# The end of an attention and spectral-filter kernel: the last output product in three rounded terms, its stores on another queue, its last block copied in two halves

## The chip, the cores and the metric

One core of a Trainium2 chip runs the whole kernel. The metric is device time in microseconds (us), from the start to the end of one execution. The names of the engines are those of the profile: PE multiplies matrices (PEld is its load of the stationary operand), DVE is the vector engine, ACT the scalar engine, POOL is GpSimd and SP is SyncE, which here only issues DMAs and waits. A trailing q (SPq, ACTq) is the engine's instruction sequencer: DMA issues, semaphore waits, register loads and branches are its work.

## What is computed

Two independent results stand side by side in the output. One is attention with 16 query heads of width 28 that share one key and one value head, over 2048 positions; the other is a 2-D FFT of a second input, a pointwise product with a filter, and the inverse FFT. The change touches only the attention's last product:

```python
scores = jnp.einsum("bhqd,bkd->bhqk", q, k) * (Dh ** -0.5)
p = _softmax(scores, axis=-1)
o = jnp.einsum("bhqk,bkd->bhqd", p, v)
return (lambda x, *d: x.transpose(*d))(o, 0, 2, 1, 3).reshape(B, S, H * Dh) @ wo
```

All data are float32. `x @ wo` has 448 rows of `wo` and 448 columns of output.

## The kernel before, in words

The 2048 query positions are cut into `NC` = 4 chunks of `CW` = 512, the 16 heads into `NG` = 4 groups of 4 heads, 32 rows a head. For each pair (chunk `c`, group `g`) PE makes scores of 16 key blocks (line 872), ACT takes the exponentials (lines 816 and 895, with DVE copying some scores out first, line 878), and PE multiplies them with the values into one PSUM bank, with the sum of the exponentials in a spare row (`flush`, line 827). When a pair is complete, DVE transposes the bank into the SBUF tile `osb` (line 831), divides by the sums (`divide`, line 713) and transposes back.

What comes next is a product with one group's rows of `wo`. PE takes float32 operands in several passes; operands of type `F32R`, a rounded float32, in one. To keep precision with rounded operands the kernel splits a tensor into a rounded part and the rounded remainder, and adds three products: high by high, low by high, high by low. `woh` and `wol` hold the two parts of `wo`, `wox` the high part for groups 1 to 3 as it belongs to the low part of the other operand (a few spare rows of it differ). `oh[c]` and `ol[c]` hold the two parts of the divided attention output. `norm` (line 715) fills them for a pair, `wo_mm` (line 730) makes the three products, and `wo_out` (line 738) copies a finished block of 128 positions by 448 columns out of PSUM and stores it to the output `oa`. For chunks 0 to 2 and for groups 0 to 2 of chunk 3 all this is spread through the main loop or done at its end.

The order of work on PE is that of the program text from line 231 on, and that of DVE and ACT from line 493 on. SP's and POOL's instructions are put in order by the framework. Waits are set by the framework too, from what the instructions read and write.

The last pair, chunk 3 and group 3, is handled by lines 907 to 934. Its part of `wo` is loaded once more, unrounded, into the tile `w3` (lines 908 and 909, from SP's queue). `flush(kept)` makes the last products with the values. DVE then divides and transposes in four blocks of 128 positions, into the tile `on` (lines 924 to 927). PE meanwhile makes the products of groups 0 to 2 for a block, nine rounded matmuls into one PSUM bank (`partial`, line 912), and adds the last group's in float32 (`final`, line 916):

```python
for k in (0, 1):
    partial(k)
for k in (2, 3):
    final(k - 2)
    partial(k)
final(2)
final(3)
```

For these four blocks `wo_out` is called with `on_act=True`: ACT copies the block (line 741) and issues the store from its own queue (line 746).

Behind this stands a block of code for inputs whose scores exceed a bound (lines 939 to 1005). It isn't entered with these inputs. Every one of the five engines loads the value `bits` into a register (line 939) and takes the branch over that code (line 940). Past it each engine has some semaphore waits (line 940 again; on SP one for each of the five DMAs that the skipped code would issue), then the end of the program (line 1123): SP waits one after another for the semaphores of all DMA queues and engines, each engine drains, and a common barrier ends the program.

Of the kernel before, what the change touches and what calls it, by code (L numbers as in the profile page):

```python
# [10 lines left out]
F32 = mybir.dt.float32  # L11
# [3 lines left out]
AF = mybir.ActivationFunctionType  # L15
ALU = mybir.AluOpType
# [4 lines left out]
S, D, H = 2048, 448, 16  # L21
DH = D // H
DF = D // 2 + 1
NG = 4
# [38 lines left out]
def kernel(ctx: ExitStack, tc: tile.TileContext, t: dict):  # L63
    nc = tc.nc
    mm = nc.tensor.matmul
# [71 lines left out]
    def fft1_a_mm(q, p):  # L137
        f, cs1 = ff[q], fc["cs1"][:113]
        pa = pair_of(bank())
        for e in range(2):  # L140
            for k, (n, o0) in enumerate(((113, 0), (112, 113))):
                for h in range(2):
                    for r in range(2):
                        r0 = 64 * h + 32 * r
                        mm(pa[r0:r0 + 32, e, o0:o0 + n], f[:, 2 * r + k, 2 * p + e, h], cs1[:, 2 * r + k, :n],  # L145
                           start=True, stop=True)
        return pa

    def fft1_a_out(q, p, pa):
        a = at1[q, p] = fp.tile([128, 2, DF], F32, name="a", tag=("pwr", "pwi")[p])  # L150
        return nc.scalar.activation(a, pa, AF.Copy)

    def fft1_b(q):
        return fft1_out(q, fft1_mm(q))
# [92 lines left out]
    with tc.tile_pool(name="w1", bufs=1) as w1:  # L247
# [37 lines left out]
        with tc.tile_pool(name="x1", bufs=2) as x1:  # L285
# [63 lines left out]
            def evac(c, g, pq):  # L349
                cs = slice(c * CW, (c + 1) * CW)  # L350
                out = nc.scalar.activation(qraw[:, g, cs], pq, AF.Copy)
                nc.vector.tensor_reduce(qmx[:, g, c:c + 1], qraw[:, g, cs], axis=AX.X, op=ALU.max,
                                        apply_absolute_value=True)
                return out
# [55 lines left out]
            for c in range(1, NC):  # L410
                for g in range(NG):
# [3 lines left out]
                    last = evac(c, g, pq)  # L415
# [43 lines left out]
        for p in range(2):  # L459
            last = fft1_a_out(6, p, fft1_a_mm(6, p))  # L460
# [7 lines left out]
        last = fft1_b(5)  # L468
# [26 lines left out]
    d, f, a, b, e, c = free  # L495
# [14 lines left out]
    ap = pools.enter_context(tc.tile_pool(name="ap", bufs=2))  # L510
    pp = pools.enter_context(tc.tile_pool(name="pp", bufs=P_BUFS))
# [25 lines left out]
    def at_once(work=640, engine="dve"):  # L537
        clock[engine] = max(clock[engine], clock["pe"] + 200) + work

    begun = []  # L540
    woh = ap.tile([128, NG, D], F32R, name="woh", bufs=1)
    wol = ap.tile([128, NG, D], F32R, name="wol", bufs=1)

    wox = ap.tile([128, NG - 1, D], F32R, name="wox", bufs=1)

    wo = {}
# [143 lines left out]
    oh, ol, osb = {}, {}, {}  # L690
# [11 lines left out]
    def divide(c, g, k=None):  # L702

        o = osb[c, g]
        sums = o.rearrange("p (b d) -> p b d", d=32)
        if not k:
            r = osb["r"] = ap.tile([128, 16], F32, name="r", bufs=1)
            nc.vector.reciprocal(r, sums[:, :, DH])
            if c == NC - 1:
                nc.vector.memset(sums[:, :, DH:], 0.0)  # L710
        s = slice(0, 16) if k is None else slice(4 * k, 4 * k + 4)
        r = osb["r"][:, s].unsqueeze(2).to_broadcast([128, s.stop - s.start, 32])
        nc.vector.tensor_tensor(sums[:, s], sums[:, s], r, op=ALU.mult)
# [21 lines left out]
                    continue  # L735
                mm(p, x[c][:, g, s], w, start=(g == 0 and n == 0), stop=(g == NG - 1 and n == 2))  # L736

    def wo_out(p, c, k, on_act=False):
        y = pp.tile([128, D], F32, name="yb", tag="p") if on_act else ap.tile([128, D], F32, name="ya")
        if on_act:  # L740
            nc.scalar.activation(y, p, AF.Copy)
        else:
            nc.vector.tensor_copy(y, p)
            at_once()
        r0 = c * CW + k * 128
        (nc.scalar if on_act else nc.sync).dma_start(t["oa"][r0:r0 + 128], y)

    wps = {}

    def wo_unit(c, k, g):  # L750
        if g == 0:
            wps[c, k] = take()
        p = wps[c, k][:, :D]
        need(("o", c, g))
        for x in (g,) if g == 0 else (g, g + NG - 1):
            need(("wo", x))
        wo_mm(p, c, k, (g,))
        passed(600 if g else 400)
        if g == NG - 1:
            wo_out(p, c, k)  # L760
            give(wps.pop((c, k)))
# [90 lines left out]
    for tokens in PLAN:  # L852
# [7 lines left out]
        for k in tokens:  # L860
# [5 lines left out]
            i, h = divmod(x[kind], 4)  # L866
# [3 lines left out]
            c, g, kc = steps[i if kind == "-" else n - 1]  # L870
# [25 lines left out]
        else:  # L896
            for h in lazy:
                p = keep[h // 2][:, h % 2]
# [6 lines left out]
        pop()  # L905

    c = NC - 1
    w3 = ap.tile([128, D], F32, name="w3", tag="ya")
    nc.sync.dma_start(w3, t["wo"][:, NG - 1])
    ws = []  # L910

    def partial(k):
        ws.append(take()[:, :D])
        wo_mm(ws[k], c, k, range(NG - 1))

    def final(k):
        p = ws[k]
        mm(p, on[:, 128 * k:128 * k + 128], w3, start=False, stop=True)
        wo_out(p, c, k, True)


    flush(kept)
    on = ap.tile([128, CW], F32, name="osb")
    for k in range(4):
        divide(c, NG - 1, k)
        s = slice(128 * k, 128 * k + 128)
        nc.vector.transpose(on[:, s], osb[c, NG - 1][:, s])
    for k in (0, 1):
        partial(k)
    for k in (2, 3):  # L930
# [6 lines that stand above are left out]
# [3 lines left out]
    with tc.If(rv > int(np.float32(BOUND).view(np.int32))), tc.tile_pool(name="g1", bufs=1) as g1:  # L940
# [31 lines left out]
        oa = t["oa"].rearrange("(n p) d -> n p d", p=128)  # L972
        with tc.For_i(0, NC, 1) as nq:
            y = g1.tile([128, 4, D], F32, name="y")
            nc.vector.memset(y, 0.0)
            with tc.For_i(0, NG, 1) as ng:
# [5 lines left out]
                for i in range(4):  # L982
# [3 lines left out]
                    with tc.For_i(0, 16, 1) as nk:  # L986
# [5 lines left out]
                        p = g1.tile([128, CW], F32, name="pe")  # L992
# [134 lines left out]
```

## Time and profile before

| quantity | value |
|---|---|
| median of 3 runs | 642.26 us |
| lowest and highest of them | 642.26 and 642.81 us |
| time of the profiled execution | 642.82 us |
| its span, first to last instruction | 641.0 us |
| granted PE clock, share of full speed | 1.000 |
| HBM read, written | 30.04 MB, 14.75 MB |

The span leaves 1.82 us of the profiled execution outside it. Times in the profile count from the start of the span. A line of the timeline or of the chain of waits starts with the start time and the duration in us. A line that lists the instructions of one source line gives their count, the shortest, median and longest duration in ns, and the start times of the first and of the last. A line of the waits gives who waited, for whom, the sum in us, the count, and the longest.

### The profile page before, as it was taken

Reading aid. Unit: us, or ns where it says so; the run is one execution under the profiler, and the core shown is the slowest. Engines: PE = TensorE matmul, PEld = TensorE weight load, DVE = VectorE, ACT = ScalarE, POOL = GpSimd, SP = SyncE. Lnnn points to the kernel's source line nnn. Section 1 sums busy time; section 2 is a strip of 40 time slices with the busy share of each in tenths; the row PEclk is TensorE's granted clock in tenths of the full one; section 3 lists DMA queues with packets and bytes.
Section 4 is the critical chain, followed back from the end, with each engine's and each line's share of the span. In section 5 each row is a group of like instructions: output and inputs, shape, how many; then the busy total and the mean of one; then the engine's idle time right before and its main releaser. Section 6 shows DMA issues by size and latency. Waiting matters only on the chain.

```text
span 641.0 us, 12024 instructions
## 1 busy us (share of the span) xinstructions
PE 635.7 (99%) x4470; PEld 381.8 (60%) x4470; DVE 372.3 (58%) x683; ACT 550.7 (86%) x1011; POOL 80.1 (12%) x150
## 2 busy tenths in 40 slices
PE   9999999999999999999999999999999999999997
PEld 6877655556555556655655566556655566556555
DVE  5999628889997934766543523264545332264521
ACT  5554999999999998988899898998999898998981
POOL 3021401011311110000120300003031100200110
PEclk9999999999999999999999999999999999999999
DMA  8755971554835521214241403123241303140001
GB/s 271 268 161 159 262 175 47 143 126 111 205 102 128 142 59 49 79 47 136 63 103 44 115 16 85 39 57 92 55 120 43 88 15 81 44 127 2 30 31 60
DMA packets 36113, 63.83 MB, mean 100 GB/s; under 512 B 7905, under 2 KB 23922, under 8 KB 35084
## 3 DMA queue, kind: packets, MB, share of 16 engines
q1 hardware_dynamic: 30832, 49.60, 28.0%
q0 software_dynamic: 4640, 12.48, 7.8%
q10 hardware_dynamic: 576, 0.92, 0.4%
q8 instruction: 36, 0.59, 0.4%
q14 instruction: 29, 0.24, 0.1%
HBM read 30.04 MB, written 14.75 MB: 70 GB/s over the span
## 4 chain that ended last, share of the span: by engine, by line
PE 98%; DMA 1%; ACT 0%; SPq 0%; issue 0%; ACTq 0%
PE s L872 31%; PE s L827 22%; PE sx L827 9%; PE s L347 6%; PE po L872 5%; PE po L827 4%; PE s L736 4%; PE sx L872 4%; PE s L145 2%; PE s L674 2%; PE s L660 2%; PE pbb L164 1%; DMA raw<-wq 1%; PE s L562 1%; PE s L561 1%; PE s L563 1%
## 5 line engine op out<-in xcount | busy, mean ns | idle before, releaser
L816 ACT ACTIVATE p<-s 128x512 f32<-128x512 f32 x650 | 345.9, 631 | 33.4 <-PE s L872 27.5
L872 PE MATMUL s<-qa,ka 128*128 128x512 f32 x798 | 236.1, 405 | 0.0
L872 PEld LDWEIGHTS s<-qa,ka 128*128 128x128 f32 x798 | 146.7, 188 | 67.7 <-issue 26.8
L878 DVE COPY k<-s 128x512 f32<-128x512 f32 x129 | 82.5, 682 | 106.6 <-PE s L872 106.6
L827 PE MATMUL s<-p,vs 128*32 128x512 f32 x1024 | 121.7, 595 | 0.0
L895 ACT ACTIVATE k<-k 128x1024 f32<-128x1024 f32 x88 | 90.3, 1108 | 0.0
L827 PEld LDWEIGHTS s<-p,vs 128*32 128x32 f32 x1024 | 30.8, 109 | 67.6 <-issue 65.6
L816 ACT ACTIVATE p<-po 128x512 f32<-128x512 f32 x89 | 56.2, 631 | 9.2 <-PE po L872 8.5
L816 ACT ACTIVATE p<-sx 128x512 f32<-128x512 f32 x85 | 53.6, 630 | 3.1 <-PE sx L872 1.9
L827 PE MATMUL sx<-p,vs 128*32 128x512 f32 x416 | 49.3, 594 | 0.0
L872 PE MATMUL po<-qa,ka 128*128 128x512 f32 x120 | 49.2, 410 | 0.0
L872 PE MATMUL sx<-qa,ka 128*128 128x512 f32 x106 | 42.4, 400 | 0.0
L700 POOL DMA_DIRECT2D ol<-ol x36 | 18.1, 510 | 135.9 <-DVE ol L723 69.0
L827 PE MATMUL s<-k,vs 128*32 128x512 f32 x256 | 33.4, 594 | 0.0
L684 POOL TENSOR_TENSOR yo<-y 128x226 f32<-128x226 f32 x16 | 9.5, 596 | 188.0 <-DVE y L680 110.9
L872 PEld LDWEIGHTS po<-qa,ka 128*128 128x128 f32 x120 | 22.5, 188 | 14.6 <-issue 9.2
L827 PEld LDWEIGHTS sx<-p,vs 128*32 128x32 f32 x416 | 12.5, 110 | 27.9 <-issue 27.6
L831 DVE STREAM_TRANSPOSE osb<-s 128x512 f32<-128x512 f32 x10 | 7.2, 715 | 37.0 <-PE s L827 37.0
L878 DVE COPY k<-po 128x512 f32<-128x512 f32 x29 | 19.8, 681 | 14.3 <-PE po L872 14.3
L827 PE MATMUL po<-p,vs 128*32 128x512 f32 x208 | 25.0, 595 | 0.0
L872 PEld LDWEIGHTS sx<-qa,ka 128*128 128x128 f32 x106 | 19.9, 188 | 6.7 <-issue 2.5
L347 PE MATMUL s<-xh,wqh 128*128 128x512 f32 x56 | 23.0, 410 | 0.1
(217 smaller groups left out, 788.1 us busy)
## 6 DMA issues: line engine op xcount, KB each, us to landing
qa<-qa SPq DMA_DIRECT2D x15, 512.0 KB
raw<-xa SPq DMA_DIRECT2D x16, 256.0 KB
xb<-xb SPq DMA_DIRECT2D x8, 512.0 KB
qa<-qh SPq DMA_DIRECT2D x64, 64.0 KB
qa<-ql SPq DMA_DIRECT2D x60, 64.0 KB
ob<-yo SPq DMA_DIRECT2D x16, 226.0 KB
t<-bs SPq DMA_DIRECT2D x16, 225.0 KB
wr<-wr POOLq DMA_DIRECT2D x16, 225.0 KB, 4.2
```

Source lines behind the costliest of these rows:

```text
L145: mm(pa[r0:r0 + 32, e, o0:o0 + n], f[:, 2 * r + k, 2 * p + e, h], cs1[:, 2 * r + k, :n], start=True, stop=True)
L347: mm(pq, w[:, j, gs], x[:, j], start=(j == 0 and n == 0), stop=(j == 3 and n == 1))
L660: mm(pz[:w, j], c2["c", q][:, j, o0:o0 + w], c2["F", q][:, j], start=True, stop=True)
L674: mm(py[:, k], z[:w, r, js], cs3[:w, k], start=True, stop=True)
L684: nc.gpsimd.tensor_tensor(yo[:, 0:2], y1[:, 0], y1[:, 1], op=ALU.add)
L700: nc.gpsimd.dma_start(ol[c][o, g].bitcast(F32), ol[c][r, 0].bitcast(F32))
L736: mm(p, x[c][:, g, s], w, start=(g == 0 and n == 0), stop=(g == NG - 1 and n == 2))
L816: nc.scalar.activation(tiles[-1][:, h % 2], sc, AF.Exp, scale=SCALE)
L827: mm(po[c, g][32 * i:32 * i + 32], vs[:, kc], ps[i // 2][:, i % 2], start=(n == 1), stop=(n == 16))
L872: begun.append(mm(sc, ka[:, kc * 128:(kc + 1) * 128], qa[c, g][:, h], start=True, stop=True))
L878: nc.vector.tensor_copy(keep[h // 2][:, h % 2], sc)
L895: nc.scalar.activation(p, p, AF.Exp, scale=SCALE)
```

## The change

Four things are different. The load of `w3` is gone. DVE, after each transpose of a 128-position block of the last pair, makes the rounded part of it in `oh[c]` and the remainder in `ol[c]`, and `final` adds three rounded products in place of one in float32. `wo_out` gets the number of the block, 1 to 4, as `last`: blocks 1 to 3 are still copied by ACT, but are stored from SP's queue. Block 4 is cut into two halves of 224 columns: ACT copies the first, which is stored from ACT's queue, DVE copies the second, which is stored from SP's queue.

```diff
-    def wo_out(p, c, k, on_act=False):
-        y = pp.tile([128, D], F32, name="yb", tag="p") if on_act else ap.tile([128, D], F32, name="ya")
-        if on_act:
-            nc.scalar.activation(y, p, AF.Copy)
-        else:
-            nc.vector.tensor_copy(y, p)
-            at_once()
+    def wo_out(p, c, k, last=0):
+        y = pp.tile([128, D], F32, name="yb", tag="p") if last else ap.tile([128, D], F32, name="ya")
         r0 = c * CW + k * 128
-        (nc.scalar if on_act else nc.sync).dma_start(t["oa"][r0:r0 + 128], y)
+        for e in ((0, 1) if last == 4 else (0,)):
+            s = slice(e * D // 2, (e + 1) * D // 2) if last == 4 else slice(0, D)
+            if last and not e:
+                nc.scalar.activation(y[:, s], p[:, s], AF.Copy)
+            else:
+                nc.vector.tensor_copy(y[:, s], p[:, s])
+                at_once()
+            (nc.scalar if last == 4 and not e else nc.sync).dma_start(t["oa"][r0:r0 + 128, s], y[:, s])
...
     c = NC - 1
-    w3 = ap.tile([128, D], F32, name="w3", tag="ya")
-    nc.sync.dma_start(w3, t["wo"][:, NG - 1])
     ws = []
...
     def final(k):
-        p = ws[k]
-        mm(p, on[:, 128 * k:128 * k + 128], w3, start=False, stop=True)
-        wo_out(p, c, k, True)
+        p, s = ws[k], slice(128 * k, 128 * k + 128)
+        h, l = oh[c][:, NG - 1, s], ol[c][:, NG - 1, s]
+        mm(p, h, woh[:, NG - 1], start=False, stop=False)
+        mm(p, l, wox[:, NG - 2], start=False, stop=False)
+        mm(p, h, wol[:, NG - 1], start=False, stop=True)
+        wo_out(p, c, k, k + 1)
...
         divide(c, NG - 1, k)
         s = slice(128 * k, 128 * k + 128)
         nc.vector.transpose(on[:, s], osb[c, NG - 1][:, s])
+        h = oh[c][:, NG - 1, s]
+        nc.vector.tensor_copy(h, on[:, s])
+        nc.vector.tensor_tensor(ol[c][:, NG - 1, s], on[:, s], h.bitcast(F32), op=ALU.subtract)
```

## The prediction, made before the changed kernel ran

> **What bounds the kernel now.** I read the page's first lines, then the chain of waits over the last 20 us, then the timeline there, and last the instructions that stand behind the program's branch.
>
> ```profile
> span 641.0 us, 12024 instructions
> PE 635.7 (99%) x4470; PEld 381.8 (60%) x4470; DVE 372.3 (58%) x683; ACT 550.7 (86%) x1011; POOL 80.1 (12%) x150
> ```
> ```profile
> 632.87 0.75 PE s L918 x2
> 633.62 1.82 PE s L736 x9
> 635.44 0.77 PE s L918 x2
> 636.21 0.02 issue
> 636.23 0.55 ACT yb L741
> 636.78 0.02 issue
> 636.80 0.34 ACTq L746
> 637.14 0.05 issue
> 637.19 0.54 ACT yb L741
> ```
> ```profile
> 635.28 1.66 PE L918 MATMUL s<-w,osb 128*128 128x448 f32 x4
> 637.76 0.34 ACTq L746 DMA_DIRECT2D oa<-yb  x1
> ```
>
> PE is busy for 99% of the span, so up to 636 us everything is PE's time. The chain shows what the change can reach: each float32 product of the last group takes 0.75 us (0.77 the next time), nine rounded ones 1.82 us. PE's last product ends at 635.28 + 1.66 = 636.94. ACT could copy block 4 then, but is issuing block 3's store until 637.14 and starts at 637.19. The last store is issued at 637.76. From there to the end there is no arithmetic left, and still 3.2 us. These are SP's:
>
> ```profile
> SPq L940 <- SPq L940: 10.2, 2, 7.3
> SPq L1123 <- DMA oa<-yb: 5.7, 2, 4.8
> ```
> ```profile
> L1123 SPq EVENT_SEMAPHORE  x4: 28/28/28, 633.8 to 634.0; - x4
> ```
>
> SP goes through its final waits in a fixed order. Four pass from 633.8 to 634.0, 0.07 us each. The next lasts 4.8 us, to 638.8, and is block 3's store; the one after 0.9 us, to 639.7, block 4's store. So a store is seen about 1.95 us after its issue began (637.76 to 639.7), and from there to the span's end it takes 641.0 - 639.7 = 1.3 us: the rest of the waits, the drains, the barrier. **The bound at the very end is the last store's landing, because SP has done everything else long before.** When did it do that?
>
> ```profile
> 620.85 1.68 SPq L687 DMA_DIRECT2D ob<-yo  x2
> ```
> ```profile
> L939 SPq TENSOR_LOAD <-bits x1: 541/541/541, 622.6 to 622.6; - x1
> L939 DVEq TENSOR_LOAD <-bits x1: 545/545/545, 629.6 to 629.6; - x1
> ```
> ```profile
> L940 POOLq COMPARE_BRANCH  x1: 54/54/54, 621.6 to 621.6; - x1
> L940 SPq COMPARE_BRANCH  x1: 50/50/50, 623.2 to 623.2; - x1
> L940 DVEq COMPARE_BRANCH  x1: 72/72/72, 630.2 to 630.2; - x1
> ...
> L940 DVEq EVENT_SEMAPHORE  x1: 21/21/21, 633.1 to 633.1; - x1
> ...
> L940 ACTq COMPARE_BRANCH  x1: 54/54/54, 638.7 to 638.7; - x1
> L940 ACTq EVENT_SEMAPHORE  x1: 17/17/17, 639.2 to 639.2; - x1
> ```
> ```profile
> L940 SPq EVENT_SEMAPHORE  x4: 17/17/17, 626.1 to 626.4; - x4
> ```
> ```profile
> L1123 POOLq DRAIN  x3: 46/108/8992, 622.0 to 640.8; - x3
> L1123 SPq DRAIN  x3: 7/7/13, 640.2 to 640.5; - x3
> ```
>
> This is the part that I take for decisive. SP's last DMA of the kernel before ends at 620.85 + 1.68 = 622.53. It then loads the register (0.54 us), branches at 623.2, and its next instruction starts only at 626.1. No transfer holds that one, since a store issued by 622.53 is seen by 624.5, and the list of waits names nobody but SP itself for it: the jump took 2.9 us. DVE shows the same, 630.2 to 633.1. ACT (638.7 to 639.2) and POOL (621.6 to 622.0) jump in 0.4 to 0.5 us. The program's end costs SP, from its last DMA issue to its first instruction behind the branch, 626.1 - 622.53 = 3.6 us. Now this lies beside PE's last 18 us and costs nothing.
>
> [...]
>
> **The change part by part.** *PE.* Nine rounded products in 1.82 us are 0.20 each; three are 0.61 against 0.75, so each of the four finals saves 0.14 us, together 0.6. PE's end moves from 636.94 to 636.35. The finals must not wait for DVE:
>
> ```profile
> 627.73 0.29 DVE L713 TENSOR_TENSOR osb<-osb,r 128x128 f32<-128x128 f32 x1
> 628.05 0.31 DVE L927 STREAM_TRANSPOSE osb<-osb 128x128 f32<-128x128 f32 x1
> ...
> 629.61 0.31 DVE L927 STREAM_TRANSPOSE osb<-osb 128x128 f32<-128x128 f32 x1
> ```
> ```profile
> L557 DVE CAST woh<-wo x4: 381/387/393, 136.1 to 168.3; 128x448 fp32r<-128x448 f32 x4
> ```
> ```profile
> 630.13 0.91 PE L918 MATMUL s<-w,osb 128*128 128x448 f32 x2
> ```
>
> *DVE, between the transposes.* A cast of 128x128 isn't in the trace: at most the 0.39 us of a 128x448 one, at least a quarter of it, 0.1; I take 0.2, as instructions a quarter as long don't get four times shorter. The subtraction has the shape of line 713, 0.29. With gaps of 0.03 a block costs 0.5 more, at most 0.75. Block 1 is ready at 628.05 + 0.31 + 0.55 = 628.9, at the most 629.1, and PE wants it at 630.13. Block 4, whose transpose ended at 629.92, comes at 632.0, at most 632.9; PE wants it after 635. PE's partials cover this with over a microsecond, so it costs nothing.
>
> *The load of w3.*
>
> ```profile
> L909 SPq DMA_DIRECT2D w<-wo x1: 376/376/376, 571.0 to 571.0; - x1
> ```
>
> It leaves SP's queue at 571 us, and what stood behind it goes 0.4 us earlier. PE is busy throughout and waits for none of it: nothing.
>
> *Copies and stores.* Block 3's products end two finals of saving earlier plus its own, at 636.21 - 0.43 = 635.78; ACT copies it from 635.8 to 636.35, and SP issues its store to 636.7. Block 4's products end at 636.35, and ACT, which no longer issues that store, is free. The ACT half comes between zero and 0.54 us; I take 0.33, nearer the whole one's half with a fixed part. ACT's store is issued from 636.75 to 637.1. DVE's half has a near row:
>
> ```profile
> 618.37 0.39 DVE L678 COPY m<-s 128x226 f32<-128x226 f32 x1 [0.78 <-PE s L674]
> ```
> ```profile
> L743 DVE COPY ya<-s x9: 619/625/625, 233.1 to 570.0; 128x448 f32<-128x448 f32 x9
> ```
> ```profile
> L746 SPq DMA_DIRECT2D oa<-ya x12: 333/348/983, 233.8 to 570.6; - x12
> ```
>
> 226 columns out of PSUM took 0.39 us, so 636.4 to 636.8; if reading one bank beside ACT slows it, at most the 0.62 of a whole block. SP's issue takes 0.35 (0.98 at the worst), and ends at 637.2. Landing 1.95 us after 636.84 would be 638.8, and if that still set the end, the span would be 0.9 shorter, 640.1.
>
> *What is late in its place.* SP now has its last DMA at the very end, so its register load, its jump and its waits follow that. 637.2 + 3.6 = 640.8 for the first instruction behind the branch. Then come its five waits of line 940 at about 0.09 us (the first four ran within 626.1 to 626.4), four and one of line 1123 at 0.07, and the part that took 1.3 us after the last landing: 640.8 + 0.45 + 0.35 + 1.3 = 642.9, less 0.1 for what rounding adds at each of these, 642.8. DVE gets the same jump: its load starts with its copy at about 636.4, and 3.5 us later (629.6 to 633.1) it is at 639.9, before SP. ACT's tail, 639.2 before, comes at 638.2.
>
> **The sum**: 642.8 against a span of 641.0, +1.8 us. The profiled execution was 642.82 us, so 644.6 by its measure; the median shown is 642.26, and 644.1 is what I expect of a median.
>
> **Rivals.** *A second wait in the split block.* If the framework holds DVE's half until ACT's half is written, because both write the tile yb, DVE starts at 636.75 in place of 636.4: 644.5. Nothing in the trace writes one tile from two engines so closely.
>
> *SP's jump is short* (the other side). [...] Then SP is behind the branch 2.4 us earlier, at 638.4, goes on to the landings at 638.8, and DVE's jump sets the end: its drain follows at 640.0, where SP's stood at 640.2 before. That is 0.2 less than now: 642.1. The point from which it decides: with SP's jump under 2.4 us the loss is too small to be told, under 0.9 us DVE's end is the later one. Against it: nothing takes out more than the load and its wait, and four stores with theirs come in, a small shift in front of a skipped body that stays as long.
>
> *Both jumps are short*, and the change does what its parts do: 0.9 less, 641.3, by landing alone. DVE's code grows by some ten instructions, but its 2.9 us are as firm as SP's.
>
> *PE waits for DVE's last block.* If partials, which read other groups of oh and ol, wait for all of DVE's new writes, PE stands from 626.4 or, if only the first final waits, from 630.1 to 632.0: the latter is 2 us on top of my sum, 646.0. The rows can't exclude it, since all four transposes of before ended at 629.92, before PE's first final.
>
> **How the numbers follow.** My forecast 0.70, the second wait 0.09, SP's jump short 0.08, both short 0.08, PE waiting 0.05. About 0.2%, 1.28 us, is what a measurement of this kernel can tell from no change: the bounds are 640.98 and 643.54. The forecast's own range: 0.25 less if the copy and the jump come at their shortest; up to 0.23 more by the copy and 0.63 by the issue; and 0.55 us between runs of before, so 643.2 to 645.1. It holds nearly all of the forecast and of the second wait, some 0.78, and by rounding I leave the rest out. Slower: 0.63 of the forecast, the second wait and PE waiting, 0.77. Within: 0.07 of the forecast, SP's short jump, and 0.02 of both short, 0.17. Faster: 0.06, both short with a run's scatter.
>
> **What would show it.** Right: in the rows of line 940 SP's branch near 637.9 and its next instruction near 640.8; SP's final waits pass without one for a store of oa; three rounded products a final in 0.6 us. DVE's branch near 637.1, and its next instruction 2.8 us behind. Wrong: SP's next instruction under a microsecond behind its branch; PE idle ahead of a final; or a wait for the last store's landing that still ends last.

## The result: 0.34% slower, and the profile after

The changed kernel takes 644.93 us (median of 7 runs, 644.02 to 645.24), the kernel before beside it 642.35 us (7 runs, 642.22 to 642.81). The ratio is 1.0034, its 95% interval 1.0025 to 1.0044. The profiled execution took 644.93 us, its span is 643.1 us.

First the page's head, and the chain of waits over the last 23 us (start, duration, what):

```profile
span 643.1 us, 12041 instructions
PE 635.0 (99%) x4474; PEld 382.5 (59%) x4474; DVE 374.9 (58%) x692; ACT 550.5 (86%) x1011; POOL 80.2 (12%) x150
```
```profile
636.25 0.36 ACT yb L744
636.61 0.02 issue
636.63 0.39 DVE yb L746
```

The chain, which before went through the products and ACT's stores, has three pieces left and stops at 637.02, six microseconds ahead of the end. It follows waits back, and what stands behind 637.02 waits for nothing that the profile can name. The timeline and the rows of the program's end show it (those rows give the count, the shortest, median and longest duration in ns, the first and last start in us):

```profile
635.63 0.97 ACT L744 ACTIVATE yb<-s 128x448 f32<-128x448 f32 x2 [1.88 <-PE s L921]
635.78 0.37 PE L921 MATMUL s<-wol,oh 128*128 128x448 f32 x1
636.21 1.18 SPq L748 DMA_DIRECT2D oa<-yb  x2
636.63 0.38 ACTq L748 DMA_DIRECT2D oa<-yb  x1
636.63 0.39 DVE L746 COPY yb<-s 128x224 f32<-128x224 f32 x1 [4.48 <-ACT yb L744]
```
```profile
L945 DVEq TENSOR_LOAD <-bits x1: 807/807/807, 636.6 to 636.6; - x1
L945 ACTq TENSOR_LOAD <-bits x1: 631/631/631, 637.0 to 637.0; - x1
L945 SPq TENSOR_LOAD <-bits x1: 642/642/642, 637.4 to 637.4; - x1
```
```profile
L946 SPq EVENT_SEMAPHORE  x5: 17/17/17, 641.0 to 641.4; - x5
...
L946 DVEq COMPARE_BRANCH  x1: 72/72/72, 637.5 to 637.5; - x1
L946 ACTq COMPARE_BRANCH  x1: 54/54/54, 637.8 to 637.8; - x1
L946 SPq COMPARE_BRANCH  x1: 50/50/50, 638.2 to 638.2; - x1
L946 ACTq EVENT_SEMAPHORE  x1: 17/17/17, 638.2 to 638.2; - x1
L946 DVEq EVENT_SEMAPHORE  x1: 21/21/21, 640.7 to 640.7; - x1
```
```profile
L1129 SPq EVENT_SEMAPHORE  x14: 17/28/28, 641.4 to 643.0; - x14
L1129 SPq DRAIN  x3: 7/7/13, 642.2 to 642.5; - x3
```

PE's last product ends at 635.78 + 0.37 = 636.15, 0.79 us earlier than before. SP's second store of the timeline's pair ends at 636.21 + 1.18 = 637.39, the register load at 638.1, SP's branch starts at 638.15, and the next instruction starts at 641.04. **That is a jump of 2.9 us with the whole machine standing behind it.** SP's final waits then run through from 641.4 to 642.1 without a stop, so no landing ends last. DVE does the same 0.4 us ahead of SP. The list of SP's waits over these 20 us names the jump as a wait of SP for itself, once and no longer twice, and no store of oa:

```profile
SPq L748 <- ACT yb L744: 13.2, 3, 9.1
SPq L946 <- SPq L946: 2.9, 1, 2.9
SPq L687 <- POOL yo L685: 0.9, 1, 0.9
SPq L1129 <- PEq L1129: 0.7, 2, 0.5
SPq L748 <- DVE yb L746: 0.4, 1, 0.4
```

### The profile page after: what moved, and what is told of

It is laid out like the page before. It is cut to its first block, busy times and chain, and to the rows that moved or that the text cites. A ratio compares the mean times of both kernels' runs of the same rounds, so it can differ in the third digit from the quotient of the medians.

```text
span 643.1 us, 12041 instructions
## 1 busy us (share of the span) xinstructions
PE 635.0 (99%) x4474; PEld 382.5 (59%) x4474; DVE 374.9 (58%) x692; ACT 550.5 (86%) x1011; POOL 80.2 (12%) x150
```

## The experiments

**The theory**: the loss is SP's jump, 2.9 us, which the new store puts behind the last copy; it depends on where in SP's code the branch lies. **The rivals**: the second wait, DVE's half behind ACT's half, is what costs; DVE's jump is the bound; the landing still ends last. Since PE's stream ends anywhere from 635.07 to 636.41 us in profiles with the same products, I read each profile by its *tail*, the time from the end of PE's last product to the span's end: 641.0 - 636.94 = 4.06 us before, 643.1 - 636.15 = 6.95 us after. A table of all tails stands at the end of this section.

### Only the place of SP's branch: 86 empty instructions

The changed kernel, with 86 empty instructions on SP while it has nothing to do, around 600 us. Everything behind them in SP's code lies 86 instructions further on; nothing else is different. (`stored` is a list that the kernel has already; `stored[-3]` is the store of `ob` at 596.5 us.)

```diff
-        nc.sync.dma_start(t["ob"][r0:r0 + 128], yo)
+        stored.append(nc.sync.dma_start(t["ob"][r0:r0 + 128], yo))
...
+    with tc.issue_after(stored[-3].ins):
+        for _ in range(86):
+            nc.sync.drain(fusable=False)
     flush(kept)
```

> The changed kernel with 86 empty drain instructions on SP, behind the store of 596.5 us, where SP idles for over 20 us. [...] Theory (SP's jump past the fallback code, 2.9 us behind its last store, sets the end): the jump falls to about 0.5 us as on ACT, SP is through 2.4 us earlier, and DVE's jump, 2.9 us long and done at 640.7, sets the end instead: span 641.5, 1.5 us less than the changed kernel, about 643.4 us. Rival (the end is late because of the two half copies and their stores, not because of the jump): no difference, 644.9 us.

Measured: 643.49 us (643.21 to 644.36), ratio 1.0017 (1.0008 to 1.0026), span 642.2, tail 5.83. The rows of the branch, which is line 949 here, and of SP's waits:

```profile
L949 SPq EVENT_SEMAPHORE  x5: 17/17/17, 638.9 to 639.2; - x5
L949 DVEq COMPARE_BRANCH  x1: 72/72/72, 637.8 to 637.8; - x1
L949 SPq COMPARE_BRANCH  x1: 50/50/50, 638.4 to 638.4; - x1
L949 DVEq EVENT_SEMAPHORE  x1: 21/21/21, 640.8 to 640.8; - x1
```
```profile
SPq L949 <- SPq L949: 0.5, 1, 0.5
```

SP's jump went from 2.9 to 0.5 us without a change in what SP does. The tail is only 1.1 us shorter. DVE's jump, which was covered by SP's, is late now: DVE comes out at 640.8, and SP can't pass its wait for DVE before. But SP isn't at that wait then. Its final waits, line 1132 here, stop behind the ninth; these are the rows of the first nine and of the next three, the wait for DVE first among the three:

```profile
L1132 SPq EVENT_SEMAPHORE  x9: 27/28/28, 639.3 to 639.8; - x9
```
```profile
L1132 SPq EVENT_SEMAPHORE  x3: 28/28/28, 641.1 to 641.2; - x3
```

The wait for DVE starts at 641.09 and lasts 28 ns, so it wasn't DVE that held SP up to there; DVE's last event, at 640.79, is 0.3 us older, and the list of SP's waits names no wait of line 1132 for DVE. What ends last in this profile is the stop, with DVE's jump 0.3 us ahead of it. The run with 88 empty instructions below has the same stop at the same wait. The median is what was expected, 643.4, but the profile's span of 642.2 is 0.7 above the 641.5 expected, so part of the hit is luck.

The same with 40 in place of 86, as a control:

> [...] Theory: SP's jump stays at 2.9 us and the time at 644.9 us. Rival (the drains themselves, or any shift of SP's code, change the end): about half of what 86 drains change.

Measured: 644.86 us (644.12 to 645.33), ratio 1.0036 (1.0023 to 1.005), tail 6.86. SP's wait for itself in line 949 is 2.8 us. So it isn't the empty instructions as such that shorten the jump, it is how far they move it. The code between the branch and its target is the same in both runs, only its place differs: 2.8 us with 40 ahead of it, 0.5 us with 86. Why the place decides, these two runs don't show.

### Telling the engines of the branch ahead of it

A program can carry a hint that a branch will be taken. Here SP gets it behind its last store of ob, DVE behind its last transpose.

```diff
+    with tc.issue_after(stored[-1].ins):
+        tc.mark_branch_hint_location("big", "LikelyTaken", engines=(mybir.EngineType.SP,))
+    with tc.issue_after(tr.ins):
+        tc.mark_branch_hint_location("big", "LikelyTaken", engines=(mybir.EngineType.DVE,))
...
-    with tc.If(rv > int(np.float32(BOUND).view(np.int32))), tc.tile_pool(name="g1", bufs=1) as g1:
+    with tc.If(rv > int(np.float32(BOUND).view(np.int32)), label="big"), tc.tile_pool(name="g1", bufs=1) as g1:
```

> [...] Theory: both jumps fall from 2.9 to about 0.5 us, and the end is set by the landing of the last half store again: issue at 637.05, seen at 639.0, end at 640.3, 2.8 us less than the changed kernel and 0.7 less than before, so 641.6 to 642.1 us. If only SP's jump were shortened, DVE's would set the end: 643.4. Rival (not the jumps): 644.9 us.

Measured: 644.63 us (643.9 to 645.27), ratio 1.0032 (1.0021 to 1.0044), tail 7.0. A miss. The hints ran (SP's at 622.48, DVE's at 631.41, 0.06 us each), but both jumps stayed. The view of the DMA queues from 623 to 636 us (packets, MB, share of the engines) shows what followed the hints:

```profile
q1 hardware_dynamic: 420, 0.67, 14.0%
q8 instruction: 1, 0.02, 0.4%
```

Code comes over two queues named "instruction"; before and after, from 595 us on, q8 has packets of 16384 bytes and q14 packets of 8192 bytes. No packet of q14 starts in this window. (It has one packet at 622.79, but so it has in the changed kernel at 622.58 and before at 622.80.) The one packet of q8 isn't new either: the changed kernel has one in the same stretch, at 634.06. So no fetch of code that the changed kernel lacks followed the hints, the jumps stayed at 2.9 us on SP and 3.1 on DVE, and the theory isn't touched by this run.

### One store of the kernel before moved to SP

The smallest part of the change that has the cost by the theory: the kernel before, with nothing different but the queue of block 4's store.

```diff
-        (nc.scalar if on_act else nc.sync).dma_start(t["oa"][r0:r0 + 128], y)
+        (nc.scalar if on_act and k < 3 else nc.sync).dma_start(t["oa"][r0:r0 + 128], y)
```

> The kernel before, with one thing of the change alone: the store of block 4 is issued by SP in place of ACT. Copies and products are as before. Theory: SP's last issue ends at about 638.1, and 5.65 us of SP's end follow (register load, jump, waits, barrier, as after the change): span 643.7, 2.7 us more than before, 645.1 us. Rival (the queue doesn't matter, the loss of the change comes from its copies): 642.4 us.

Measured: 644.94 us (644.43 to 645.53), ratio 1.0038 (1.0025 to 1.0052), tail 643.1 - 636.65 = 6.45 us.

```profile
637.47 0.33 SPq L746 DMA_DIRECT2D oa<-yb  x1
```
```profile
L940 SPq EVENT_SEMAPHORE  x5: 17/17/17, 641.0 to 641.4; - x5
L940 DVEq COMPARE_BRANCH  x1: 72/72/72, 630.0 to 630.0; - x1
L940 DVEq EVENT_SEMAPHORE  x1: 21/21/21, 633.1 to 633.1; - x1
L940 SPq COMPARE_BRANCH  x1: 50/50/50, 638.5 to 638.5; - x1
```

**This one edit has all of the change's loss.** DVE is out of its jump at 633.1, there is no split block and no second wait, and SP's jump alone sets the end.

### The other way round: the change without SP's stores, and without the split

First the changed kernel with all five stores of the last blocks on ACT's queue, the split kept:

```diff
-            (nc.scalar if last == 4 and not e else nc.sync).dma_start(t["oa"][r0:r0 + 128, s], y[:, s])
+            (nc.scalar if last else nc.sync).dma_start(t["oa"][r0:r0 + 128, s], y[:, s])
```

> The changed kernel with all five stores of the last chunk on ACT's queue; rounded products and the two half copies stay. SP issues nothing late. Theory: SP's jump goes back under cover at 623 us. Block 3's store holds ACT for 0.35 us again, so ACT's half is copied to about 636.95 and DVE's half from then on; DVE's register load starts with its copy, its jump ends 4.1 us later at 641.1, and sets the end: span 641.9, 0.9 more than before and 1.2 less than the changed kernel, 643.3 us. If DVE's jump cost nothing, the last landing would set it: 640.6, 642.0 us. Rival (the loss comes from the half copies): 644.9 us.

Measured: 643.27 us (642.89 to 644.21), ratio 1.0013 (1.0004 to 1.0022), span 642.0, tail 5.71. SP is past its branch early, as before. What ends last is in the list of SP's waits, DVE's jump:

```profile
SPq L1129 <- DMA oa<-yb: 2.1, 2, 1.6
SPq L1129 <- DVEq L946: 1.4, 1, 1.4
```
```profile
L946 DVEq COMPARE_BRANCH  x1: 72/72/72, 637.9 to 637.9; - x1
L946 DVEq EVENT_SEMAPHORE  x1: 21/21/21, 640.9 to 640.9; - x1
```

Then also without DVE's half, so that of the change only the rounded products remain (besides the line above, `wo_out(p, c, k, 1)` in `final`, with which ACT copies block 4 whole):

> The kernel before with the rounded products alone: ACT copies all four blocks whole and stores them from its own queue. No late work on SP or DVE. Theory: PE ends 0.6 us earlier, block 3's store still holds ACT for 0.35 us, the last store is issued at 637.3 in place of 637.76, and the end is its landing: 0.45 us less than before, 642.0 us. Rival (the casts on DVE between the transposes, or the products, are what the change loses by): over 643 us.

Measured: 642.07 us (641.34 to 642.86), ratio 0.9991 (0.9982 to 1.0), span 640.3, tail 4.28. With both jumps off the end, the landing of the last store is the bound again, as it was before:

```profile
SPq L1129 <- DMA oa<-yb: 5.4, 1, 5.4
```
The rounded products, which the prediction rated at a gain, gain a little at most; the stores and the split turn it round.

### SP's stores without the split, and with the branch moved

Blocks 1 to 3 stored by SP, as changed; block 4 copied whole by ACT and stored by ACT.

```diff
-        for e in ((0, 1) if last == 4 else (0,)):
-            s = slice(e * D // 2, (e + 1) * D // 2) if last == 4 else slice(0, D)
+        for e in (0,):
+            s = slice(0, D)
```

> The changed kernel with block 4 left whole, copied by ACT and stored from ACT's queue; blocks 1 to 3 are stored by SP as in the change. SP's last issue is then block 3's, which ended at 636.54 in the changed kernel, 0.85 us before that of the half block. DVE's last work is at 632. Theory: SP's 5.65 us follow its last issue, so the span is 642.2, 0.9 us less than the changed kernel: 643.9 us, or 643.6 counted from before. Rival (the last landing sets the end, and SP's jump is beside it): the last store is issued at 636.8 and the span is 640.1, 641.6 us.

Measured: 643.97 us (642.85 to 644.22), ratio 1.0025 (1.0016 to 1.0034), tail 5.99. SP's jump, 2.8 us, starts behind block 3's store and still sets the end:

```profile
SPq L946 <- SPq L946: 2.8, 1, 2.8
```

With 88 empty instructions on SP as in the first experiment:

> The last kernel (block 4 whole on ACT, blocks 1 to 3 stored by SP) with 88 empty drains on SP at 596.5 us, so that SP's branch stands where it jumped in 0.45 us before. Theory: SP is behind its branch by 638, DVE long before, and the landing of block 4's store, issued at about 636.8, sets the end: span 640.1, 0.9 us less than the kernel before, 641.5 us, and the fastest of all. Rival: as without the drains, 643.6 to 643.9 us.

Measured: 642.56 us (641.48 to 643.07), ratio 1.0004 (0.9995 to 1.0013), tail 640.2 - 635.42 = 4.78 us. SP's jump was 0.5 us, as expected, and the kernel faster by 1.4 us than without the empty instructions, but it missed what I had expected of it by 1 us in the median. SP's waits at the very end show a stop that I had not reckoned with. Here are the rows of these waits from 638.2 to 638.6, and from 638.6 to 639.5:

```profile
L1132 SPq EVENT_SEMAPHORE  x5: 28/28/28, 638.3 to 638.5; - x5
```
```profile
L1132 SPq EVENT_SEMAPHORE  x3: 28/28/28, 639.1 to 639.3; - x3
```

Between the fifth and the sixth lie 0.6 us, and the list of waits names nobody for it. With the four that came earlier these five are the first nine final waits, so it is the stop of the run with 86 again; in both runs SP has run 610 instructions ahead of its branch. To see whether this too is a matter of place, I took 14 of the 88 out again:

```diff
-        for _ in range(88):
+        for _ in range(74):
```

> The kernel of the run before with 88 empty instructions on SyncE (block 4 copied and stored whole by ScalarE, blocks 1 to 3 stored by SyncE), with 74 in place of the 88. There SyncE's short jump was followed by one more stop of 0.6 us, between its waits at 638.53 and 639.15, beside a fetch of 8192 bytes of code at 638.14. Theory (SyncE's last waits ran over the end of a code block that wasn't there yet, and 14 fewer instructions ahead of it put that end behind the program's last instruction): the jump stays at 0.5 us, the stop between those two waits is gone, and the end is 0.6 us earlier: some 642.0 us where 88 gave 642.56, and 2.2 us plus 1.35 us from the last store's issue to the span's end. Rival (those waits stand for something that the profile doesn't name, such as a landing): the stop stays, 642.5 us. Against both: if 74 are too few for the short jump, it is 2.9 us and the time 644.0 us, as without empty instructions.

Measured: 641.58 us (640.96 to 642.69), ratio 0.999 (0.9981 to 0.9999), tail 639.9 - 635.62 = 4.28 us. The jump stays at 0.5 us and the stop is gone, eight waits in a row:

```profile
L1132 SPq EVENT_SEMAPHORE  x8: 28/28/28, 638.5 to 639.0; - x8
```

The stop had added 0.5 us to the tail. The medians are 0.98 apart, more than it explains (the profiled execution of the 88 took 642.00, well below its median); the interval of each ratio reaches 0.0009, some 0.6 us, to either side, which covers the rest. That place in the code decides over the stop is shown; that code was late there is only argued, since no packet of q14 starts inside it (the last ahead of it ran from 638.14 to 638.56). This is the fastest kernel of the study, below the one before by 0.1%, with an interval that just stays below 1.

The packets of q14 also tell a long jump of SP's from a short one. In the three kernels in which SP jumps early, with no other engine's long jump beside it (before, stores on ACT, rounded products alone), one packet lies inside the jump. The view of the DMA queues from 623.2 to 626.1 us, in the kernel before, has it:

```profile
q14 instruction: 1, 0.01, 1.5%
```

It runs from 624.14 to 624.86, and SP's next instruction starts at 626.09. In the short jumps of the runs with 88 and 74, 636.48 to 636.97 and 636.67 to 637.16, no packet of q14 starts. So the long jump goes with a fetch of code and the short one without. That the packet holds the jump's own target the trace doesn't say.

### Why DVE's half waits for ACT's half

The changed kernel with the two halves of block 4 in two SBUF tiles:

```diff
-        y = pp.tile([128, D], F32, name="yb", tag="p") if last else ap.tile([128, D], F32, name="ya")
+        ys = [pp.tile([128, D], F32, name="yb", tag="p") if last else ap.tile([128, D], F32, name="ya")]
+        ys += [pp.tile([128, D], F32, name="yb", tag="p")] if last == 4 else []
...
+            y = ys[e]
```

> The changed kernel with one line more: the two halves of block 4 are written to two SBUF tiles, so that only the PSUM tile that they read is shared. Theory (the half on VectorE waits for ScalarE's half because both read the same PSUM tile): VectorE's half still starts at ScalarE's end, 0.48 us behind the last product's end, SyncE's issue and the end stay where they were, 644.9 us. Rival (the reason given in the prediction, that both write the one tile yb): VectorE's half starts 0.1 us behind the product's end, SyncE issues at 0.5 us behind it where it was 0.9, and with the 2.9 us jump the span is 0.4 us shorter, 642.7 us, the time 644.5 us.

Measured: 644.9 us (644.5 to 645.59), ratio 1.0041 (1.0027 to 1.0055), tail 6.78. DVE still starts as ACT ends, at 635.31 + 0.96 = 636.27:

```profile
635.31 0.96 ACT L746 ACTIVATE yb<-s 128x448 f32<-128x448 f32 x2 [1.88 <-PE s L923]
636.30 0.39 DVE L748 COPY yb<-s 128x224 f32<-128x224 f32 x1 [4.47 <-ACT yb L746]
```

So the tile written isn't the reason. What the halves still share is the tile that they read, in PSUM, the memory into which PE writes its products. That leaves it as the reason by argument; no run here gave each half a PSUM tile of its own.

With block 4 copied whole by DVE, nothing of ACT's reads the tile that DVE reads:

```diff
-        for e in ((0, 1) if last == 4 else (0,)):
-            s = slice(e * D // 2, (e + 1) * D // 2) if last == 4 else slice(0, D)
-            if last and not e:
+        for e in (0,):
+            s = slice(0, D)
+            if last and last < 4:
...
-            (nc.scalar if last == 4 and not e else nc.sync).dma_start(t["oa"][r0:r0 + 128, s], y[:, s])
+            nc.sync.dma_start(t["oa"][r0:r0 + 128, s], y[:, s])
```

> The changed kernel with block 4 copied whole by VectorE and stored from SyncE's queue, in place of the two halves. Theory (the half's wait for ScalarE's half comes from both reading one PSUM tile; a copy out of another product's tile than ScalarE's waits for its own product alone): VectorE's copy starts some 0.05 us behind the last product's end and not behind a copy of ScalarE's, lasts 0.62 us, SyncE issues at about 0.68 us behind the product's end where it was 0.90 in the changed kernel, and with the long jump of 2.9 us behind it the span is about 642.9 us, the time 644.7 us (0.2 below the changed kernel). Rival (any copy of VectorE's at this place waits for ScalarE's copy before it): starts at the end of ScalarE's copy of block 3, and the same time to 0.05 us, since that copy ends at the same moment; only the waits tell these two apart. What the split buys is then nothing: expected slower than the kernel before by 0.3%.

Measured: 643.81 us (643.32 to 644.72), ratio 1.0026 (1.0016 to 1.0035), tail 641.5 - 635.07 = 6.43 us.

```profile
634.55 0.55 ACT L744 ACTIVATE yb<-s 128x448 f32<-128x448 f32 x1 [1.88 <-PE s L921]
635.17 0.62 DVE L746 COPY yb<-s 128x448 f32<-128x448 f32 x1 [4.11 <-PEq L946]
```

The whole copy on one engine is ready 0.73 us behind the last product, the two halves one after the other were ready 637.02 - 636.15 = 0.87 us behind it. So the split made block 4 later than no split. ACT's copy of block 3 ends at 635.10, 0.07 ahead of DVE's start, so this run doesn't tell the theory from its rival (that any copy of DVE's at this place waits for ACT's copy before it), and neither does the run with two tiles, where ACT's copy before is the half of the same PSUM tile. As a general rule the rival fails: in the main loop of the changed kernel DVE starts to copy a score tile at 101.91 us, while ACT reads another one from 101.62 to 102.22. For this place it stays open. Of the 0.5 us that the tail is shorter than the changed kernel's, 0.14 is the copy, and 0.4 are SP's register load (0.49 for 0.64) and jump (2.65 for 2.89, from the start of the branch).

### All tails

Times in us, each from its profiled execution; the jump is SP's wait behind its branch, as the list of waits gives it.

| kernel | last product's end | span | tail | SP's jump | what ends last |
|---|---|---|---|---|---|
| before | 636.94 | 641.0 | 4.06 | 2.9, early | landing |
| changed | 636.15 | 643.1 | 6.95 | 2.9 | SP's jump |
| 86 empty instructions | 636.37 | 642.2 | 5.83 | 0.5 | a stop of SP, 0.3 us behind DVE's jump |
| 40 empty instructions | 636.24 | 643.1 | 6.86 | 2.8 | SP's jump |
| hints | 636.30 | 643.3 | 7.00 | 2.9 | SP's jump |
| before, block 4's store on SP | 636.65 | 643.1 | 6.45 | 2.5 | SP's jump |
| changed, stores on ACT | 636.29 | 642.0 | 5.71 | early | DVE's jump |
| rounded products alone | 636.02 | 640.3 | 4.28 | early | landing |
| block 4 whole on ACT | 636.41 | 642.4 | 5.99 | 2.8 | SP's jump |
| the same, 88 empty | 635.42 | 640.2 | 4.78 | 0.5 | landing and a stop of SP |
| the same, 74 empty | 635.62 | 639.9 | 4.28 | 0.5 | landing |
| block 4 whole on DVE | 635.07 | 641.5 | 6.43 | 2.6 | SP's jump |
| two SBUF tiles | 635.82 | 642.6 | 6.78 | 2.8 | SP's jump |

The tails fall into three groups by what ends last, and the medians follow them: 641.6 to 642.6 us with the landing, 643.3 and 643.5 with DVE's jump or the stop close behind it, 643.8 to 644.9 with SP's.

## Why the prediction was right, step by step

**The step that carried it** was that SP's register load, jump and remaining waits would follow its last store. From that issue's end to the first instruction behind the branch it said 3.6 us; it was 641.04 - 637.39 = 3.65. From there to the end it said 2.0; it was 643.1 - 641.04 = 2.06. The experiments show the cause from both sides: moving one store brings the loss (644.94 us), moving SP's branch by 86 instructions cuts the jump from 2.9 to 0.5 us.

**The finals.** In the kernel before, a float32 product stands in the trace as two matmuls, eight for the four products, 0.75 us a product:

```profile
L918 PE MATMUL s<-w,osb x8: 537/537/539, 630.1 to 636.4; 128*128 128x448 f32 x8
```

A rounded product is one matmul. Three rounded products were to take 0.61 us; their rows say 0.2 from one start to the next, 0.6 for three (the last final's first product starts at 635.4, its third at 635.8), and no final waited:

```profile
L919 PE MATMUL s<-woh,oh x4: 367/367/367, 629.9 to 635.4; 128*128 128x448 f32 x4
L921 PE MATMUL s<-wol,oh x4: 363/363/368, 630.3 to 635.8; 128*128 128x448 f32 x4
```

PE's end came 0.2 us earlier than said (636.15 for 636.35), which lies within what the stream's end differs by from profile to profile; that it went this way is luck.

**DVE's new work** was rated at 0.5 us a block, hidden:

```profile
L932 DVE CAST oh<-osb x4: 226/228/229, 628.2 to 631.6; 128x128 fp32r<-128x128 f32 x4
L933 DVE TENSOR_TENSOR ol<-osb,oh x4: 293/293/294, 628.5 to 631.9; 128x128 fp32r<-128x128 f32 x4
```

0.23 + 0.29, the last done at 632.2 (said: 632.0), over three microseconds ahead of its product. The rival in which PE waits for it is refuted. ACT's tail at 638.2 was as said.

**Mis-sized: DVE's half.** The forecast let it start with the product's end, at 636.4. It waited for ACT's half and started at 636.63, 0.48 us behind the product's end. This is the second wait that I gave 0.09 as a rival, at 644.5. It happened, but not for the reason I gave: the tile yb written isn't it, as the run with two tiles shows, and the PSUM tile read is what is left, by argument. It costs 0.4 us on the path to SP's store. Less PE's earlier end of 0.2, and with the 0.1 by which the two stretches of SP's end came out longer, that is the 0.3 us by which the span, 643.1, is above the sum, 642.8.

**Mis-sized: the way from the sum to the median.** I took 0.5 us off, since the profiled execution of before lay that much above its median. That of after is the median. The two together are the 0.8 us by which 644.93 lies above 644.1; it is inside the range. The bounds of the range don't come out of the terms that the prediction names for them: all taken together, they give 643.3 and 645.5 where it says 643.2 and 645.1. The measured time lies inside both.

**The rival "SP's jump is short"** named the right next bound, DVE's jump, as the run with the stores on ACT shows; with 86 empty instructions DVE's jump is 0.3 us from it, behind a stop of SP's that no rival had. Its price, 642.1, was too low: with the 86 it was 643.49. It had DVE out of the jump at 639.9, and it was 640.8. Half of that is the second wait with DVE's start, the rest DVE's register load, 0.81 us where before's row had 0.55, and a jump of 3.0 us where it had 2.9. SP's stop adds 0.3. Why the load took longer stays open.

**"Both jumps are short", 641.3,** couldn't be made with the split; DVE's jump was never short in any run. Without DVE on the path, the 74 empty instructions gave 641.58.

## What to carry to other kernels

Before moving a last DMA to another queue, look what else that engine has to do between its last issue and the program's end: register loads, branches over code that isn't entered, waits; an engine that did these early did them for nothing, and here they came back at full price when its last issue moved to the end, 3.65 us from there to the first instruction behind the branch where before had 3.6. A chain of waits that stops well ahead of the span's end, as here at 637.02 of 643.1 us, leaves open what ends last; look at the rows of the branch and the events behind it. Before a block is cut in two for two engines, see whether both halves come out of one PSUM tile: here the two ran one after the other (the first to 636.61 us, the second from 636.63), also with two SBUF tiles to write to (to 636.27, from 636.30).

## What the runs showed of the hardware that wasn't expected

- SP's taken branch over the same distance costs 2.5 to 2.9 us or 0.5 us, by where it lies in SP's code: 40 empty instructions ahead of it changed nothing, 74, 86 and 88 made it short. DVE's took 2.8 to 3.4 us in every run, by the starts in its rows.
- SP's long jump goes on after the packet of code inside it has landed. In the kernel before the packet ends 1.2 us ahead of SP's next instruction. From 638 to 641.1 us of the changed kernel, where DVE jumps too, q14 carries three packets, 638.80 to 639.64, while SP's next instruction starts at 641.04. What fills the remaining 1.2 and 1.4 us isn't shown.

```profile
q14 instruction: 3, 0.02, 2.5%
```

- A hint of the branch, given 16 us ahead on SP, was followed by no packet of code that the other kernels lack, and shortened nothing.
- SP's final waits can stop too: 0.6 us with 88 empty instructions and 1.3 us with 86, behind the same wait, and not with 74. That it is a fetch of code is only argued.
- One register's load takes 0.48 us (ACT before) to 0.82 us (DVE in the run with 88), depending on engine and run, and stands on the path as well.
